# Attention scores at full height in two passes instead of half height in three, a rotated key copy and a joint last transpose

## The chip, the core and the metric

One core of a Trainium2 chip runs the whole program in one launch. The metric is the device time of one execution in microseconds (us). Engines: PE (TensorE, matmuls), DVE (VectorE), ACT (ScalarE), POOL (GpSimd), and SP (SyncE), which issues all DMAs here.

## The reference

Attention with a threshold, then two MLPs over the same 2304 tokens, all in fp32 (`q`, `k`, `v` are 4 x 8 x 576 x 64, the MLP weights 512 x 2048 and 2048 x 512):

```python
scores = scale * np.matmul(q, k.transpose(0, 1, 3, 2))
thresh = np.max(scores, axis=-1, keepdims=True) - tau
scores = np.where(scores >= thresh, scores, -1000000000.0)
...
attn = attn / (np.sum(attn, axis=-1, keepdims=True) + 1e-09)
return np.matmul(attn, v).astype(np.float32)
...
h = x @ w_in
g = np.maximum(h, 0.0) + alpha * np.minimum(h, 0.0)
...
h = x @ w_in
g = h - np.tanh(h)
```

The first MLP has the leaky step, the second `h - tanh(h)`; each ends with `g @ w_out`.

## The kernel before

**Precision.** Most matmuls take operands in a shorter format (`fp32r`). A value is written as a high part and a low part (the rest), and a product of two values is a sum of products of parts. The MLPs use three of the four products (L849 to L920).

**Visits.** Attention runs in 64 visits: for each of 4 batches, 256 queries of each of 8 heads (block 0), then the next 256 with the heads in reverse (block 1). The last 64 queries of two heads form one "left" tile, handled after every second visit of block 1 (`attend_left`, L723). `prep` (L407) loads and splits keys, values and queries of a visit; `attend` (L642) does the rest:

- *Scores* (`scores`, L649). The head dimension is 64, so a matmul contracts over 64 of 128 rows. The host lays keys and queries out twice, on rows 0 to 63 and 64 to 127; the upper half computes query tile 0 into the PSUM tile `sc0`, the lower half query tile 1 into `sc1`. A pass is 2 column chunks (320 and 256 keys) by 2 halves. Visits whose keys came with one of the first 22 visits (`raw`, `RAW` = 22) make a single pass in plain fp32; the other 42 make three passes (high x high, low x high, high x low), 12 matmuls.
- *Softmax* (`softmax`, L523): per tile row maximum (DVE), threshold, exponential (ACT), mask and sum (DVE), reciprocal, and a normalisation on ACT, DVE or POOL. The weights are in the tile `e`, 128 x 576, one per query tile.
- *Transposes* (`turned`, L581): four 128 x 128 transposes of a tile's first 512 keys into `pt` (`turn`, L587), copied out as high part (ACT) and low part (DVE); one transpose of the last 64 keys (`turn_last`, L591) into the first 128 columns of `sc0` or `sc1` (of `hp` in the first 8 visits).
- *Products* with the values (L668), then the sums that form the MLP's input.

The left tiles of raw heads use a two-head key tile and a zero-padded query tile `qz` (L736); the other left tiles use `qc` (L738), 8 matmuls on all 128 rows.

**MLPs.** Nine blocks of 256 tokens per layer, eight pairs of 128-wide hidden slices each: `h_pair` (L846) and `acc_pair` (L899). Layer 1 of a block begins when its eight visits are done and runs between later visits; layer 2 follows alone.

**Order.** All steps are recorded in a plan (`Plan`, L74) with engines, assumed costs, a rank, and what they read, write and take. `order` (L113) simulates the engines and issues, each time, the step that can start first; among steps ready at the same time the lower rank goes first. Where several engines are allowed, `ACT_PEN`, `DVE_PEN` and `POOL_PEN` are added to that engine's start. Each engine then runs its list in that order. 140 filler steps of two matmuls (`warm`, L974) have the last rank.

Ranks come from a visit's place times `TA` plus an offset by kind of step (`OFF`, L60):

```python
add({"PE": 1.27 if raw(k) else 1.09}, rank + OFF["S"], scores, ...
add({"PE": 0.434}, rank + OFF["T"], turn, [e0, ("const", 2), ROOM], [("pt", 0)], [("pt", 0)])
add({"PE": 0.07}, rank + OFF["T"], turn_last, [e0, ("const", 2), ROOM], [p5k], bank)
```

Of the kernel before, what the change touches and what calls it, by code (L numbers as in the profile page):

```python
# [22 lines left out]
P = 128  # L23
BLK = 256
# [5 lines left out]
KW, VW = S, 5 * D  # L30
QW = (BLK, BLK + D)
QH = P + D
# [5 lines left out]
TA = 13.2318  # L38
PA, PB = 19.265, 1.663
MLP_PE = 552.3152  # L40
MLP_G = -221.5201
PREP = 5.2216
# [4 lines left out]
POOL_PEN = 0.1711  # L47
ACT_PEN = 0.2206
# [6 lines left out]
XR = 58.2596  # L55
# [3 lines left out]
DVE_PEN = 0.7265  # L59
OFF = {"S": -61.66, "M": -127.29, "TH": -411.91, "E": -10.04, "X": -74.89, "R": -109.09, "N": 45.44, "T": 228.67, "H": -130.72, "L": -184.11, "AV": 77.62, "XC": -91.16, "XH": 81.73}  # L60
# [3 lines left out]
    "rkv": 1, "rq": 2, "ks": 3, "qs": 2, "vs": 3, "e": 3, "st": 2, "eT5": 1, "xt": 1, "rw": 4, "raw0": 2, "raw1": 4, "tw": 2,  # L64
# [165 lines left out]
def attention_mlp_mlp(ctx: ExitStack, tc: tile.TileContext, kv, q0, q1, tau, w1i, w1o, alpha, w2i, w2o, out):  # L230
# [30 lines left out]
    qc = tpool.tile([P, 2, P], F32R, name="qc")  # L261
    qz = tpool.tile([P, P], F32, name="qz")
# [115 lines left out]

# [28 lines left out]
    def prep(v, rank):  # L407
# [21 lines left out]

        def load_whole_k(e):  # L430
            T[ks] = take(tpool, ks, [P, 2, S], F32R, "ks", BUFS["ks"]).bitcast(F32)
            e.dma_start(out=T[ks][:, 0], in_=kv[b, h][:, :KW])

        def load_whole_v(e):
            x = take(tpool, vs, [P, 2, 5, D], F32, "vs", BUFS["vs"])
            e.dma_start(out=x[:, 0], in_=kv[b, h][:, KW:].rearrange("p (c d) -> p c d", c=5))
            T[vs] = x.rearrange("p a c d -> p c a d")
# [4 lines left out]

        def k_hi(e):
            copy(e, take(tpool, ks, [P, 2, S], F32R, "ks", BUFS["ks"])[:, 0], T[rkv][:, :KW])

        def k_lo(e):
            sub(e, T[ks][:, 1], T[rkv][:, :KW], T[ks][:, 0])
# [11 lines left out]
        def q_hi(e):  # L459
            x = take(tpool, qs, [P, 2, P], F32R, "qs", BUFS["qs"])  # L460
            copy(e, x.bitcast(F32)[:, 0] if raw(k) else x[:, 0], T[rq][:, :P], scale=qscale)

        def scaled_lo(e, lo, x, hi):
            e.scalar_tensor_tensor(
                out=lo, in0=x, scalar=qscale[P - lo.shape[0]:], in1=hi.bitcast(F32), op0=ALU.mult, op1=ALU.subtract
            )

        def q_lo(e):
            scaled_lo(e, T[qs][:, 1], T[rq][:, :P], T[qs][:, 0])
# [3 lines left out]

        half = HALVES[h % 2] if raw(k) else slice(0, P)

        def left_hi(e):
            copy(e, qz[half, col] if raw(k) else qc[:, h % 2, col], T[rq][half, P:], scale=qscale[half])

        def left_lo(e):
            x = qc[D:, h % 2, col]  # L480
            scaled_lo(e, x, T[rq][D:, P:], x)

        def load_two(e):
            x = take(tpool, kab, [P, KW + VW], F32, "rkv", BUFS["rkv"])
            for a in range(2):
                e.dma_start(out=x[HALVES[a], :KW], in_=kv[b, h + a][HALVES[a], :KW])

        add({"SYNC": rate * QH}, rank - 6, load_q, [ROOM], [rq], takes=[("rq", rq)], lag=DMA_LAG)
        k_raw, v_raw = (*rkv, 0), (*rkv, 1)
        if new:  # L490
# [10 lines left out]
            if not raw(k):  # L501
                add(any_of(0.58, 0.37, 0.64), rank, k_hi, [k_raw, ROOM], [(*ks, 0)], takes=[("ks", ks)])
                add(either(0.68, 1.42), rank, k_lo, [k_raw, (*ks, 0), ROOM], [(*ks, 1)])
        add({"ACT": 0.28}, rank, q_hi, [rq, ("const", 0), ROOM], [(*qs, 0)], takes=[("qs", qs)])
        if not raw(k):
            add({"DVE": 0.26}, rank, q_lo, [rq, (*qs, 0), ROOM], [(*qs, 1)])
        if qb:
            lc = ("qz" if raw(k) else "qc", 0, h % 2)
            if raw(k) and h % 2 == 0:
                add({"SYNC": rate * KW}, rank - 6, load_two, [ROOM], [(*kab, 0)], takes=[("rkv", kab)], lag=DMA_LAG)  # L510
            add({"ACT": 0.24}, rank, left_hi, [rq, ("const", 0), ROOM], [lc])
            if not raw(k):
                add({"DVE": 0.2}, rank, left_lo, [rq, ROOM], [lc])
# [9 lines left out]
    def softmax(tile, n, slots, rank):  # L523
# [4 lines left out]
        st = ("st", tile)  # L528
# [9 lines left out]
        def row_exp(e, j, s):  # L538
            e.activation(  # L539
                out=take(tpool, ("e", tile, j), [P, S], F32, "e", BUFS["e"]), in_=x(s), func=AF.Exp, bias=T[st][:, 0, j:j + 1], scale=1.0  # L540
            )

        def row_mask(e, j, s):
            w_ = T["e", tile, j]
# [10 lines left out]
        def normalise(e, j):  # L555
            w_, r = T["e", tile, j], T[st][:, 3, j:j + 1]
# [12 lines left out]
        add({"DVE": 0.13}, rank + OFF["TH"], threshold, [*[(*st, 0, j) for j in js], ("const", 0), ROOM], [(*st, 1)])  # L569
        for j, s in enumerate(slots):  # L570
            both = [("sc", s, 0), ("sc", s, 1)]
            ej = ("e", (tile, j))
            add({"ACT": 0.64}, rank + OFF["E"], lambda e, j=j, s=s: row_exp(e, j, s), [("sc", s, "s"), (*st, 0, j), ROOM], [ej], both, takes=[("e", ej)])
# [3 lines left out]
        for j in js:  # L577
            add({"ACT": 0.66, "DVE": 0.37, "POOL": 0.73}, rank + OFF["N"], lambda e, j=j: normalise(e, j), [(*st, 3), ROOM], [("e", (tile, j))])


    def turned(tile, j, s, rank, g, g5, w, left, half):  # L581

        cols = slice(0, P) if left else slice(j * P, (j + 1) * P)
        p5k, p5, bank = (("sc", s, "p5"), sc[s][:D, :P], [("sc", s, 0)]) if left or tile >= H else (("hp", s), hp[:D, s, :P], [("hp", 0)])
        e0 = ("e", (tile, j))

        def turn(e):  # L587
# [10 lines left out]
        def hi_last(e):  # L598
            if g5 not in T:
                take(tpool, g5, [P, BLK], F32R, "eT5", BUFS["eT5"])  # L600
            x = T[g5][half, cols].bitcast(F32) if w else T[g5][:D, cols]
            copy(e, x, p5)

        def lo_last(e):
            sub(e, T[g5][D:P, cols], p5, T[g5][:D, cols])

        def hi(e):
            if g not in T:
# [4 lines left out]
            if w:  # L613
                copy(e, x[:, :, cols].bitcast(F32), pt)
            elif left:
                copy(e, parts(x.rearrange("p c s -> p (c s)"), 0), pt.rearrange("p c (a s) -> p (c a) s", a=2))
            else:
                copy(e, x[:, :, cols], pt)

        def lo(e):  # L620
# [3 lines left out]
            else:  # L624
                sub(e, T[g][1][:, :, cols], pt, T[g][0][:, :, cols])

        first = j == 0
        add({"PE": 0.434}, rank + OFF["T"], turn, [e0, ("const", 2), ROOM], [("pt", 0)], [("pt", 0)])
        add({"PE": 0.07}, rank + OFF["T"], turn_last, [e0, ("const", 2), ROOM], [p5k], bank)
# [457 lines left out]
```

## Time and profile before

| | |
|---|---|
| median of 3 runs (lowest to highest) | 1180.67 us (1180.38 to 1181.76) |
| the profiled execution | 1180.95 us |
| its span (first to last instruction) | 1179.2 us |
| busy: PE, DVE, POOL, ACT | 1150.1, 678.1, 602.9, 575.0 us |
| chain that ended last, largest shares | PE 78%, DVE 11%, ACT 4% |
| DMA | 82.32 MB, mean 70 GB/s |

A busy time is the union of an engine's instructions, and idle time is put down to what ended it. Recorded durations of neighbouring matmuls overlap: the time that one takes of PE is the distance from its start to the next one's start, not its duration. Weight loads are a row of their own (PEld). Rows merge equal instructions that follow each other (x12) and name the first one's shape.

### The profile page before, as it was taken

What the parts mean: (1) busy time and instruction counts of PE and PEld (TensorE: products, weight loads), DVE (VectorE), ACT (ScalarE), POOL (GpSimd) and SP (SyncE); (2) the same over time, 40 slices, a digit from 0 to 9 for tenths busy, and PEclk for the clock granted to TensorE, in tenths of its full rate; (3) what the DMA queues carried; (4) which work ended last, traced back from release to release, by engine and by line L of the source; (5) the groups of instructions that cost most, each with busy time, mean ns of one, the idle gap of its engine ahead of it and who ended that gap; (6) DMA issues with size and microseconds to landing.
All of it is one profiled execution on the core that took longest, in us unless ns stands there. A gap on an engine that the chain in (4) does not pass through costs nothing.

```text
span 1179.2 us, 22125 instructions
## 1 busy us (share of the span) xinstructions
PE 1150.1 (98%) x8620; PEld 1049.2 (89%) x8620; DVE 678.1 (58%) x1388; ACT 575.0 (49%) x1132; POOL 602.9 (51%) x640
## 2 busy tenths in 40 slices
PE   9999999999999999999999999999999999999998
PEld 7777789899889898898998999998998999999997
DVE  5888887878877888878788685764111111111110
ACT  5877775666666656666665464564111111111111
POOL 3566655535556445555355377887344344344332
PEclk9999999999999999999999999999999999999999
DMA  6545432202122201121111153352011010010000
GB/s 192 181 151 165 150 103 73 58 24 60 39 59 90 58 25 55 43 91 55 42 41 55 41 186 134 127 162 90 1 36 37 1 37 27 11 36 7 13 19 18
DMA packets 51913, 82.32 MB, mean 70 GB/s; under 512 B 14688, under 2 KB 30048, under 8 KB 51808
## 3 DMA queue, kind: packets, MB, share of 16 engines
q1 hardware_dynamic: 51808, 80.91, 22.3%
q8 instruction: 68, 1.11, 0.4%
q14 instruction: 37, 0.30, 0.1%
HBM read 70.92 MB, written 9.96 MB: 69 GB/s over the span
## 4 chain that ended last, share of the span: by engine, by line
PE 78%; DVE 11%; ACT 4%; issue 3%; POOL 2%; DMA 1%; SPq 0%; ACTq 0%; DVEq 0%; POOLq 0%
PE hp L857 30%; PE acc L910 17%; PE acc L918 13%; PE sc L655 4%; PE pt L589 4%; PE sc L681 3%; DVE e L545 3%; DVE eT L285 2%; DVE st L533 1%; PE sc L592 1%; PE sc L771 1%; DVE st L550 1%; PE acc L673 1%; PE acc L976 1%; DMA rw<-in_w1i_dram 1%
## 5 line engine op out<-in xcount | busy, mean ns | idle before, releaser
L857 PE MATMUL hp<-x,ihi 128*128 128x256 f32 x2304 | 426.7, 285 | 1.0 <-POOL x L285 0.3
L857 PEld LDWEIGHTS hp<-x,ihi 128*128 128x128 f32 x2304 | 358.4, 189 | 9.3 <-issue 0.9
L857 PE MATMUL hp<-x,ilo 128*128 128x256 f32 x1152 | 324.0, 281 | 0.0
L876 DVE TENSOR_TENSOR mr<-hp,mr 128x512 f32<-128x512 f32 x72 | 49.8, 692 | 327.0 <-ACT mr L869 326.9
L857 PEld LDWEIGHTS hp<-x,ilo 128*128 128x128 f32 x1152 | 217.7, 189 | 0.0
L282 POOL TENSOR_SCALAR gh<-mr 128x512 fp32r<-128x512 f32 x100 | 63.3, 633 | 299.4 <-DVE mr L876 215.9
L285 POOL TENSOR_TENSOR gl<-mr,gh 128x512 fp32r<-128x512 f32 x144 | 192.5, 1337 | 21.2 <-ACT gh L280 13.6
L869 ACT ACTIVATE mr<-hp 128x512 f32<-128x512 f32 x72 | 43.1, 598 | 299.1 <-PE hp L857 295.5
L918 PE MATMUL acc<-gh,ohi 128*128 128x256 f32 x576 | 170.5, 296 | 0.0
L918 PE MATMUL acc<-gl,ohi 128*128 128x256 f32 x576 | 162.2, 282 | 0.0
L918 PE MATMUL acc<-gh,olo 128*128 128x256 f32 x576 | 161.9, 281 | 0.0
L533 DVE TENSOR_REDUCE st<-sc 128x1 f32<-128x576 f32 x144 | 106.3, 753 | 38.6 <-PE sc L655 23.1
L545 DVE SCALAR_TENSOR_TENSOR e<-sc,st,e 128x576 f32<-128x576 f32 x144 | 116.3, 814 | 12.3 <-ACT e L539 4.3
L539 ACT ACTIVATE e<-sc,st 128x576 f32<-128x576 f32 x144 | 105.2, 735 | 19.0 <-DVE st L533 16.9
L910 PE MATMUL acc<-ohi,gl 128*128 128x512 f32 x288 | 113.9, 395 | 0.0
L910 PE MATMUL acc<-olo,gh 128*128 128x512 f32 x288 | 113.8, 395 | 0.0
L910 PE MATMUL acc<-ohi,gh 128*128 128x512 f32 x288 | 113.5, 394 | 0.0
L918 PEld LDWEIGHTS acc<-gh,ohi 128*128 128x128 f32 x576 | 109.1, 189 | 1.8 <-issue 1.3
L918 PEld LDWEIGHTS acc<-gl,ohi 128*128 128x128 f32 x576 | 108.9, 189 | 0.1
L918 PEld LDWEIGHTS acc<-gh,olo 128*128 128x128 f32 x576 | 108.6, 189 | 0.0
L280 ACT ACTIVATE e<-e,st 128x576 f32<-128x576 f32 x97 | 72.9, 770 | 61.1 <-DVE st L553 60.1
L280 ACT ACTIVATE eT<-pt 128x512 fp32r<-128x512 f32 (+1 forms) x144 | 85.4, 593 | 30.6 <-PE pt L589 26.4
(89 smaller groups left out, 1953.0 us busy)
## 6 DMA issues: line engine op xcount, KB each, us to landing
rkv<-in_kv_dram SPq DMA_DIRECT2D x36, 288.0 KB, 2.8
rw<-in_w1i_dram SPq DMA_DIRECT2D x16, 512.0 KB, 4.5
rw<-in_w1o_dram SPq DMA_DIRECT2D x16, 512.0 KB, 4.2
rw<-in_w2i_dram SPq DMA_DIRECT2D x16, 512.0 KB, 4.6
rw<-in_w2o_dram SPq DMA_DIRECT2D x16, 512.0 KB, 3.4
rkv<-in_kv_dram SPq DMA_DIRECT2D x44, 160.0 KB, 2.8
ks<-in_kv_dram SPq DMA_DIRECT2D x20, 288.0 KB, 2.9
rq<-in_q_dram SPq DMA_DIRECT2D x160, 32.0 KB, 2.1
```

Of the source, the lines that this page charges most:

```text
L280: e.activation(out=out_, in_=in_, func=AF.Copy, **({} if scale is None else {"scale": scale}))
L282: e.tensor_scalar(out=out_, in0=in_, scalar1=1.0, scalar2=1.0, op0=ALU.mult, op1=ALU.mult)
L285: e.tensor_tensor(out=out_, in0=in_, in1=hi.bitcast(F32), op=ALU.subtract)
L533: e.tensor_reduce(out=T[st][:, 0, j:j + 1], in_=x(s), axis=AX.X, op=ALU.max, negate=True)
L539: e.activation(out=take(tpool, ("e", tile, j), [P, S], F32, "e", BUFS["e"]), in_=x(s), func=AF.Exp, bias=T[st][:, 0, j:j + 1], scale=1.0)
L545: e.scalar_tensor_tensor(out=w_, in0=x(s), scalar=T[st][:, 1, j:j + 1], in1=w_, op0=ALU.is_ge, op1=ALU.mult, accum_out=T[st][:, 2, j:j + 1])
L589: e.transpose(pt[:, c, :], T["e", tile, j][:, c * P:(c + 1) * P], ident)
L655: e.matmul(sc[j][:, 192:192 + S][:, c], lhsT=q_[p], rhs=k_[p, c], start=(n == 0), stop=(n == len(ops) - 1))
L857: e.matmul(hp[:, k, :], lhsT=weight(l, "i", part, f // 4)[:, c, (f % 4) * P:(f % 4 + 1) * P], rhs=T[f"x{x}", m][:, c, :], start=(n0 + n == ...
L876: e.tensor_tensor(out=T[r], in0=hp, in1=T[r], op=ALU.subtract)
L910: e.matmul(acc[t], lhsT=g[:, k, t * P:(t + 1) * P], rhs=w, start=(f == 0 and n == 0), stop=(f == NF - 1 and n == 2),)
L918: e.matmul(acc[t][:, (c % 2) * BLK:(c % 2 + 1) * BLK], lhsT=w[:, c * P:(c + 1) * P], rhs=g[:, k, :], start=(f == 0 and n == 0 and c % 2 == ...
```

## The change

**Scores of the 42 later visits.** The key tile no longer holds high and low parts side by side (`[P, 2, S]`) but stacked: high part on rows 0 to 63, low part on rows 64 to 127 (`k_lo` overwrites the lower half). A matmul on all 128 rows with the query's high part in both halves gives high x high plus high x low; a second pass with its low part gives the other two products. A query tile takes two passes of two chunks, 4 matmuls, and is a step of its own; a visit has 8 instead of 12. The query's high and low parts are formed for 256 columns instead of 128.

**Rotated keys.** The key tile has 640 columns: the last 64 keys, then all 576. Tile 1 of the queries reads columns 0 to 575, so its scores begin with the last 64 keys; tile 0 reads columns 64 to 639. The weights of both are neighbours in one tile `e` of 1152 columns, and the two pieces with the last 64 keys lie side by side: one 128-column transpose turns both. It needs both normalisations, and always goes to `sc0` (or `hp`). This holds for all 64 visits. The key load has a second DMA for the rotated 64 columns (for 56 loads), and the `e` buffers go from three of 576 columns to two of 1152.

**Left tiles.** Raw ones put their query tile behind the keys in the same buffer (four `memset`s on POOL, no `qz`); the others have stacked parts, still 8 matmuls.

**Ranks and assumed costs** are new, `ACT_PEN` becomes 0. By the two orders 89 of the copies of `gh` go from POOL to ACT (ACT 44 to 133, POOL 100 to 11), and some 50 other copies; DVE keeps 1246 instructions.

```diff
-TA = 13.2318
-PA, PB = 19.265, 1.663
...
-ACT_PEN = 0.2206
+TA = 16.6305
+PA, PB = 26.706, 2.665
...
+ACT_PEN = 0
...
+        def fill_k(e, x):
+            e.dma_start(out=x[:, D:KW], in_=kv[b, h][:, :S])
+            e.dma_start(out=x[:, :D], in_=kv[b, h][:, S - D:S])
...
         def k_lo(e):
-            sub(e, T[ks][:, 1], T[rkv][:, :KW], T[ks][:, 0])
+            sub(e, T[ks][D:], T[rkv][D:, :KW], T[ks][D:])
...
         def q_lo(e):
-            scaled_lo(e, T[qs][:, 1], T[rq][:, :P], T[qs][:, 0])
+            scaled_lo(e, T[qs][:, 1], T[rq][:, :BLK], T[qs][:, 0])
...
         def turn_last(e):
-            e.transpose(p5, T["e", tile, j][:, 4 * P:], ident)
+            e.transpose(p5, T[ek][:, 4 * P:4 * P + rows], ident)
...
-        add({"PE": 0.434}, rank + OFF["T"], turn, [e0, ("const", 2), ROOM], [("pt", 0)], [("pt", 0)])
-        add({"PE": 0.07}, rank + OFF["T"], turn_last, [e0, ("const", 2), ROOM], [p5k], bank)
...
+        for j in range(n):
+            add({"PE": 0.438}, rank + OFF["T"], lambda e, j=j: turn(e, j), [(*ek, j), ("const", 2), ROOM], [("pt", 0)], [("pt", 0)])
...
+        add({"PE": 0.111}, rank + OFF["T"], turn_last, [*[(*ek, j) for j in range(n)], ("const", 2), ROOM], [p5k], bank)
...
-                    for j, p in enumerate(HALVES):
-                        e.matmul(sc[j][:, 192:192 + S][:, c], lhsT=q_[p], rhs=k_[p, c], start=(n == 0), stop=(n == len(ops) - 1))
...
+        def scores(e, j):
+            for part in range(2):
                 for c in CHUNKS:
+                    e.matmul(
+                        sc[j][:, 192:192 + S][:, c], lhsT=T["qs", v][:, part, j * P:(j + 1) * P],
+                        rhs=T["ks", k][:, (1 - j) * D:][:, c], start=(part == 0), stop=(part == 1),
+                    )
```

PE, scores of a later visit. Before (L655; `sc_90` and `sc_91` are the PSUM tiles `sc0` and `sc1`, L918 is layer 1 of the MLP); the last four rows come three times in all:

```order
L918 MATMUL acc_92<-gh,olo_1849 128x256
L655 MATMUL sc_90<-ks,qs 128x320 [waits DVE_49]
L655 MATMUL sc_91<-ks,qs 128x320 [waits DVE_49,Activation_49]
L655 MATMUL sc_90<-ks,qs 128x256
L655 MATMUL sc_91<-ks,qs 128x256
```

Now, for another later visit (L689; `sc_89` and `sc_90` are `sc0` and `sc1`, L721 ends the products of an earlier visit, L896 is layer 1):

```order
L721 MATMUL sc_89<-eT_2958,vs 128x256
L689 MATMUL sc_89<-ks,qs 128x320
L689 MATMUL sc_89<-ks,qs 128x256
L689 MATMUL sc_89<-ks,qs 128x320
L689 MATMUL sc_89<-ks,qs 128x256
L689 MATMUL sc_90<-ks,qs 128x320 [waits DVE_49]
L689 MATMUL sc_90<-ks,qs 128x256
```

The two tiles' matmuls no longer alternate, and each tile waits for its own bank.

PE, transposes of the first visit. Before (L589 is `turn`, L592 `turn_last`, L976 the fillers):

```order
L589 MATMUL pt<-ident,e 128x128 [waits Activation_49]
L589 MATMUL pt<-ident,e 128x128 x3
L592 MATMUL hp<-ident,e 64x128
L976 MATMUL acc_93<-qc 128x256 x2
L592 MATMUL hp<-ident,e 64x128 [waits Activation_49]
L976 MATMUL acc_93<-qc 128x256 x6
L589 MATMUL pt<-ident,e 128x128 [waits Activation_49]
L589 MATMUL pt<-ident,e 128x128 x3
```

Now (L615 is `turn`, L618 `turn_last`, L1014 the fillers):

```order
L615 MATMUL pt<-ident,e 128x128 [waits Activation_49]
L615 MATMUL pt<-ident,e 128x128 x3
L618 MATMUL hp<-ident,e 128x128 [waits Pool_49]
L1014 MATMUL acc_92<-qc 128x256 x8
L615 MATMUL pt<-ident,e 128x128 [waits Activation_49]
L615 MATMUL pt<-ident,e 128x128 x3
```

One last-key transpose is left, with the second tile's normalisation (here on POOL) as its wait. In the new order it stands between the two tiles' transposes in 52 of 64 visits, in 24 of them directly behind the first tile's.

SP, the first loads. Before (L420 queries, L432 keys, L436 values, L322 weights of layer 1):

```order
L949 DMA tau_sb<-in_tau_dram 128x1
L973 DMA alpha_sb<-in_alpha_dram 128x16x1
L420 DMA rq<-in_q_dram 64x128 x2
L432 DMA ks<-in_kv_dram 128x576
L436 DMA vs<-in_kv_dram 128x320
L322 DMA rw<-in_w1i_dram 128x1024 x2
```

Now (L421 queries, L427 and L428 keys, L442 values, L320 weights):

```order
L988 DMA tau_sb<-in_tau_dram 128x1
L421 DMA rq<-in_q_dram 64x128 x2
L427 DMA ks<-in_kv_dram 128x576
L428 DMA ks<-in_kv_dram 128x64
L442 DMA vs<-in_kv_dram 128x320
L1011 DMA alpha_sb<-in_alpha_dram 128x16x1
L421 DMA rq<-in_q_dram 64x128 x2
L427 DMA ks<-in_kv_dram 128x576
L428 DMA ks<-in_kv_dram 128x64
L442 DMA vs<-in_kv_dram 128x320
L320 DMA rw<-in_w1i_dram 128x1024 x2
```

The first weights now stand behind the loads of two visits.

## Rows read from the trace of the kernel before

**Rows 1.** The page, busy time of PE and the granted clock in 40 slices.

```profile
PE 1150.1 (98%) x8620; PEld 1049.2 (89%) x8620; DVE 678.1 (58%) x1388; ACT 575.0 (49%) x1132; POOL 602.9 (51%) x640
...
PEclk9999999999999999999999999999999999999999
```

**Rows 2.** Busy time in four stretches: us, then each engine (instructions), clock, DMA.

```profile
0.00:140.00 140.00, 135.25 (x918) 106.09 (x918) 108.97 (x205) 101.28 (x208) 80.02 (x91) 1.00 0.55 167
140.00:224.00 84.00, 81.75 (x653) 73.98 (x653) 67.73 (x148) 57.59 (x120) 47.49 (x53) 1.00 0.30 90
224.00:674.00 450.00, 433.79 (x3684) 409.97 (x3684) 364.90 (x868) 282.37 (x585) 230.88 (x279) 1.00 0.18 52
674.00:1179.00 505.00, 499.29 (x3371) 459.19 (x3369) 136.56 (x169) 133.77 (x221) 244.51 (x218) 1.00 0.17 55
```

**Rows 3.** Groups by form: count, busy us, mean ns; idle us before them, and releasers.

```profile
L589 PE MATMUL pt<-ident,e 128*128 128x128 f32 x576 | 88.9, 277 | 7.3 <-ACT e L280 4.7 <-POOL e L560 1.2 <-ACT eT L280 0.5
...
L589 PEld LDWEIGHTS pt<-ident,e 128*128 128x128 f32 x576 | 64.4, 140 | 17.5 <-ACT e L280 8.8 <-issue 2.4 <-POOL e L560 2.4
...
L592 PE MATMUL sc<-ident,e 128*64 128x128 f32 x128 | 31.5, 280 | 8.5 <-ACT xt L280 5.9 <-DVE pair L801 0.9 <-DVE xt L695 0.3
...
L592 PEld LDWEIGHTS sc<-ident,e 128*64 128x64 f32 x128 | 12.9, 110 | 16.9 <-ACT xt L280 12.0 <-DVE pair L801 1.5 <-ACT e L280 1.2
```

**Rows 4.** Stretches again, first L976 alone, then L655 alone.

```profile
0.00:140.00 140.00, 43.19 (x280) 37.77 (x280) 1.00 0.55 167
...
0.00:140.00 140.00, 17.39 (x112) 9.78 (x112) 1.00 0.55 167
```

**Rows 5.** Chain that ended last: start us, length us, what; one row of layer 1.

```profile
677.31 2.84 PE hp L857 x24
```

**Rows 6.** PE in order of time around one score block: start us, length us.

```profile
266.38 0.28 PE L918 MATMUL acc<-gh,olo 128*128 128x256 f32 x1
266.58 1.07 PE L655 MATMUL sc<-ks,qs 64*128 64x320 f32 x12
267.58 0.38 PE L918 MATMUL acc<-gh,ohi 128*128 128x256 f32 x1
267.80 0.28 PE L918 MATMUL acc<-gl,ohi 128*128 128x256 f32 x1
```

**Rows 7.** PE in order of time around one block of L741.

```profile
258.57 0.28 PE L918 MATMUL acc<-gh,olo 128*128 128x256 f32 x1
258.69 1.23 PE L741 MATMUL sc<-ks,qc 128*128 128x320 f32 x8
259.76 0.40 PE L857 MATMUL hp<-x,ihi 128*128 128x256 f32 x2
```

**Rows 8.** PE in order of time around two last-key transposes in a row.

```profile
421.58 0.28 PE L857 MATMUL hp<-x,ilo 128*128 128x256 f32 x1
421.70 0.38 PE L592 MATMUL sc<-ident,e 128*64 128x128 f32 x2
421.84 0.48 PE L857 MATMUL hp<-x,ihi 128*128 128x256 f32 x2
422.16 0.28 PE L857 MATMUL hp<-x,ilo 128*128 128x256 f32 x1
```

**Rows 9.** SP's issues and PE at the start, in order of time.

```profile
4.12 0.59 SPq L432 DMA_DIRECT2D ks<-in_kv_dram  x1
...
7.48 1.24 PE L655 MATMUL sc<-ks,qs 64*128 64x320 f32 x8 [0.50 <-DMA ks<-in_kv_dram]
```

**Rows 10.** Groups by form, the low part of q on DVE, two shapes.

```profile
L464 DVE SCALAR_TENSOR_TENSOR qs<-rq,qscale,qs 128x128 fp32r<-128x128 f32 x42 | 18.9, 450 | 2.8 <-ACT qs L280 2.8
...
L464 DVE SCALAR_TENSOR_TENSOR qc<-rq,qscale,qc 64x64 fp32r<-64x64 f32 x24 | 8.7, 364 | 0.8
```

**Rows 11.** Groups by form, the normalisation on ACT and on POOL.

```profile
L280 ACT ACTIVATE e<-e,st 128x576 f32<-128x576 f32 x97 | 72.9, 770 | 61.1 <-DVE st L553 60.1
...
L560 POOL TENSOR_SCALAR e<-e,st 128x576 f32<-128x576 f32 x47 | 36.4, 774 | 46.9 <-DVE st L553 44.6 <-PE acc L673 1.9 <-DMA rkv<-in_kv_dram 0.4
```

More of the change, by code (lines that the diff above doesn't have):

```diff
@@ L54 @@
 GRP = 2
-XR = 58.2596
+XR = 138.8108
 FLEX = 1
@@ L526, in x, with weights @@
             return sc[s][:, 192:192 + S]
-        st = ("st", tile)
+        st, ek = ("st", tile), ("e", tile)
+        def weights(j):
+            return T[ek][:, j * S:(j + 1) * S]
         def row_max(e, j, s):
@@ L538, in row_exp @@
         def row_exp(e, j, s):
-            e.activation(
-                out=take(tpool, ("e", tile, j), [P, S], F32, "e", BUFS["e"]), in_=x(s), func=AF.Exp, bias=T[st][:, 0, j:j + 1], scale=1.0
-            )
+            if not j:
+                take(tpool, ek, [P, 2 * S], F32, "e", BUFS["e"])
+            e.activation(out=weights(j), in_=x(s), func=AF.Exp, bias=T[st][:, 0, j:j + 1], scale=1.0)
         def row_mask(e, j, s):
-            w_ = T["e", tile, j]
+            w_ = weights(j)
             e.scalar_tensor_tensor(
@@ L577, in softmax, with turned, cols, turn @@
         for j in js:
[L578 to L587, printed above, removed]
+            add({"ACT": 0.66, "DVE": 0.37, "POOL": 0.73}, rank + OFF["N"], lambda e, j=j: normalise(e, j), [(*st, 3), ROOM], [(*ek, j)])
+    def turned(tile, slots, rank, g, g5, w, left, half):
+        n, s, ek = len(slots), slots[0], ("e", tile)
+        rows = n * D
+        p5k, p5, bank = (("sc", s, "p5"), sc[s][:rows, :P], [("sc", s, 0)]) if left or tile >= H else (("hp", tile % 2), hp[:rows, tile % 2, :P], [("hp", 0)])
+        def cols(j):
+            return slice(j * P, (j + 1) * P)
+        def turn(e, j):
+            x = T[ek][:, j * (S + D):][:, :4 * P]
             for c in range(4):
-                e.transpose(pt[:, c, :], T["e", tile, j][:, c * P:(c + 1) * P], ident)
+                e.transpose(pt[:, c, :], x[:, c * P:(c + 1) * P], ident)
         def turn_last(e):
-            e.transpose(p5, T["e", tile, j][:, 4 * P:], ident)
+            e.transpose(p5, T[ek][:, 4 * P:4 * P + rows], ident)
         def parts(x, n):
@@ L971, in attention_mlp_mlp @@
     add({"DVE": 0.3}, -100, scales, [], [("const", 0)])
-    add({"POOL": 0.46}, 0, clear, [], [("const", 1)] + [(x, 0, a) for x in ("qc", "qz") for a in range(2)])
+    add({"POOL": 0.46}, 0, clear, [], [("const", 1)] + [("qc", 0, a, part) for a in range(2) for part in range(2)])
     add({"SYNC": 0.3}, -1, lambda e: e.dma_start(out=alpha_sb, in_=alpha.rearrange("(f p) -> p f", p=P)), [], [("alpha", 0)], lag=2.5)
```

186 lines of the change are left out of this document (101 added, 85 removed).

## The prediction

> **What bounds the kernel now.** First the page's busy shares and slices: TensorE (PE) is busy 1150.1 of 1179.2 us, 98%, at a granted clock of nine tenths or more in every slice, so at its upper level of 2.4 GHz throughout [rows 1]. Then the stretches: PE is full in all four, and the nearest other engine is VectorE (DVE), 364.9 of 450 us (81%) between 224 and 674 us, where the attention visits run between the matmuls of layer 1 [rows 2]. So time is gained by fewer PE microseconds or fewer PE waits. PE idles 29.1 us in all; the transposes account for over half of it: 8.5 us ahead of the 64-column ones (L592) and 7.3 us ahead of the 128-column ones (L589) [rows 3].
>
> One exception: 280 filler matmuls (L976), all before 140 us, keep PE busy while the visits wait for other engines [rows 4]. Their number is fixed, so PE work saved among them need not shorten anything. 112 recorded score matmuls lie there, at 8 a visit 14 of the 22 early visits.
>
> PE's durations of one instruction overlap, so I price PE work by distances between starts. The step of an ordinary 256-column matmul is 2.84/24 = 0.118 us [rows 5].
>
> **Score blocks, 42 of 64 visits.** (The 22 early visits keep their single pass; their blocks are the same size.) Now a block is 12 matmuls on half the rows. From the last matmul ahead of one (266.38) to the second behind it (267.80) are 1.42 us; two ordinary steps are 0.236, so the block costs 1.184 us [rows 6]. The twelve run as six pairs, but the block shows a penalty at both edges: its first matmul starts 0.20 us after the one ahead, and the second behind it 0.22 us after the first, where a step is 0.118. The new block is 8 matmuls on all rows, four of 320 and four of 256 columns. The leftover rows' scores (L741) have exactly that form today: 258.57 to 259.76 is 1.19 us, less one step 1.07 us [rows 7]. Gain 0.114 us, times 42: **4.8 us**. Bounds: the block may lose its good fit when split into two halves of four (nothing gained, 0), or save what the rows say; nothing in them gives more.
>
> The Trainium skill has a rule against this. "TensorEngine Tiling (Array Packing)", section "Theoretical Speedup", promises up to twice the speed for a contraction of 64 rows or fewer, so by it giving up the half-height form is a loss (rival 4 has the time). The same page's "Key Properties" says that a switch of mode drains the engine; the two edges agree with that, and the block measured in place, 1.184 us against 1.07, decides.
>
> **Last-key transposes, 64 visits.** A full visit has two 64-column transposes (L592), in future one of 128 columns; the order has 144 such instructions before and 80 after. Two in a row: from 421.58 to 422.16 are 0.58 us, less three steps of 0.118 leaves 0.226, or 0.113 us each [rows 8]. The new one loads 128 columns of weights, 0.140 against 0.110 us [rows 3]; that load lies beside the matmul ahead, so I add nothing, with 0.03 x 64 = 1.9 us as the bound. All 64 would give 7.2 us; the 14 visits among the fillers I leave out, so 50 x 0.113 = **5.6 us**.
>
> **Waits at that transpose.** PE idles 8.5 us ahead of the 128 L592 that write the score banks, mostly released by ScalarE (ACT) [rows 3]: 0.066 us each. Of these 56 go (the other 16 become 8), which would save 3.7. But each remaining one needs both halves of the weights normalised, and behind it on PE's queue stand fillers or MLP matmuls and the other half's transposes. I take half, **1.9 us**; the ends are a gain of 8.5 and the loss in the first rival.
>
> **Queues at the start.** Each key load gains a second, 64-column DMA on SyncE (SP). The alpha load moves behind the first visit, and the first w1i load behind the second visit's four. A key load holds SP 0.59 us, and the first scores waited for exactly this DMA [rows 9]. The later alpha load gives some of that back. I add **0.5 us**. If the later weights reach the end the price is the second visit's five issues, at 0.59 each some 3 us; but the first MLP matmul still stands behind nine visits in both orders, and from the eighth weight piece on the loads stand behind about the same visits. Lower end 0.
>
> **Moved or lengthened elsewhere, taken as nothing.** On DVE the low part of q is 256 columns instead of 128 (42 times). From 64 rows by 64 columns to 128 by 128 the same operation goes from 364 to 450 ns [rows 10], so 64 more columns are 86 ns and 128 more some 0.17 us: 7.2 us on DVE in a stretch with 85 us free. GpSimd (POOL) subtracts half as many key rows but 11% more columns; it has over 200 us free in that stretch. The shift from POOL to ACT (89 copies of gh among others) fills an engine with 168 us free from 224 to 674 and 371 afterwards [rows 2]. The cover in each case is PE's backlog of MLP matmuls: 786 layer-1 matmuls before and 810 now, at 0.118 us some 93 and 96 us, stand behind the last attention work in the order. Without it, these would surface as PE waits (second rival). Splitting the scores per tile lets slot 0's maximum start half a block sooner; that shortens a chain that PE mostly does not wait for, so nothing.
>
> **Sum.** The profiled execution took 1180.95 us (span 1179.2 and 1.75 around it), 0.28 above the median of 1180.67. 1180.95 - 4.8 - 5.6 - 1.9 + 0.5 = 1169.15; against the median **1168.9 us**. This case by itself: 1160 (all transposes count, every L592 wait goes) to 1175 (no gain in waits, 3 us lost at the start, longer weight loads).
>
> **Rivals.**
> 1. *Slower: the single transpose waits for the second half.* In 52 of 64 visits the new order puts it between the two halves' transposes. A normalisation lasts 0.770 us on ACT or 0.774 on POOL [rows 11]; when one engine does both, the second half is ready 0.77 us after the first, while the first half's four transposes take 0.44 (four at 0.11). That is a wait of 0.33 us, times 52 = 17 us: 1180.7 - 4.8 - 5.6 + 0.5 + 17.2 = 1188. It decides from a mean of 0.19 us per visit. For: 24 of them stand directly behind the first half's transposes. Against: in the others matmuls stand between, and normalisations run on two engines at once. 0.08.
> 2. *The gain turns into idle time.* If the visits are paced by the softmax chain on DVE, the stretch stays 450 us and PE waits instead. Only the eight visits between fillers and 224 us gain 0.113 each, 0.9: 1180.7 + 0.5 - 0.9 = 1180.3. For: 81% DVE, and 7 us more. Against: PE itself waits for it rarely [rows 3]. 0.06.
> 3. *The new order also removes waits.* If the 15.8 us ahead of both kinds of transposes vanish instead of 1.9, 1180.7 - 4.8 - 5.6 - 15.8 + 0.5 = 1155. For: slots are free separately, and the weights' buffers hold two whole visits instead of one and a half. Against: the producers are as busy as before. 0.14.
> 4. *Slower: half-height pairs are cheaper than full height.* If each of the six pairs cost one full-height step of 1.07/8 = 0.134 us [rows 7], the block would cost 0.80 us and the change would add 0.27, times 42 = 11.3 us: 1180.7 - 5.6 - 1.9 + 0.5 + 11.3 = 1185. The block measured in place, edges and all, speaks against it [rows 6]. 0.02. This is what the Trainium skill's rule above would do here.
>
> **How the numbers follow.** A measurement of this kernel tells about 0.2%, 2.4 us, from no change. My forecast has 0.70. Faster: forecast and rival 3, 0.84. Same: rival 2, 0.06. Slower: rivals 1 and 4, 0.10. The range 1157 to 1178 takes in the forecast's own bounds and most of rival 3, and leaves out rivals 1, 2 and 4 and the end of 3, about 0.19.
>
> **What would show it.** Right: a non-early score block of 1.07 us without longer steps at its edges, 80 last-key transposes at 0.11 us, PE idle time at or below 29 us, attention ending some 10 us earlier and everything after 674 us merely shifted. Wrong: idle time ahead of the new transpose released by a normalisation (rival 1), idle time spread over the score blocks' successors with DVE near 90% (rival 2), or blocks above 1.15 us (rival 4).

## The result, and the profile after the change

| | before | after |
|---|---|---|
| median of the comparison (lowest to highest) | 1181.17 us (1180.38 to 1181.76) | 1169.38 us (1168.69 to 1170.11) |
| ratio, 95% interval | | 0.9901 [0.9884, 0.9918] |
| profiled execution, span | 1180.95, 1179.2 us | 1169.88, 1168.1 us |
| PE busy, and idle (span less busy) | 1150.1, 29.1 us | 1141.2, 26.9 us |

The time is 11.8 us shorter; 1168.9 was forecast. First the page of the changed kernel, busy time (share of the span, instructions) and granted clock; it answers to [rows 1].

```profile
PE 1141.2 (98%) x8388; PEld 1051.9 (90%) x8388; DVE 662.9 (57%) x1388; ACT 663.6 (57%) x1277; POOL 525.5 (45%) x498
...
PEclk9999999999999999999999999999999999999999
```

PE has 8.9 us less work and 2.2 us less idle time. DVE has 15 us less, with the same 1388 instructions. The stretches, as in [rows 2] (us, then PE, PEld, DVE, ACT, POOL, clock, DMA):

```profile
0.00:140.00 140.00, 131.51 (x887) 102.27 (x887) 106.52 (x202) 105.48 (x213) 69.67 (x80) 1.00 0.58 171
...
224.00:674.00 450.00, 437.74 (x3567) 425.93 (x3568) 362.50 (x877) 318.62 (x647) 222.54 (x240) 1.00 0.23 65
```

Groups by form on PE, as in [rows 3] (count, busy us, mean ns, idle us ahead of them and releasers). L615 answers to L589, L618 to L592, L689 to the later visits' part of L655.

```profile
L615 PE MATMUL pt<-ident,e 128*128 128x128 f32 x576 | 88.6, 276 | 6.4 <-ACT e L278 2.2 <-ACT eT L278 2.1 <-DVE eT L283 1.4
L689 PE MATMUL sc<-ks,qs 128*128 128x320 f32 x168 | 49.8, 322 | 3.4 <-DVE xt L734 2.3 <-DVE e L565 0.9 <-ACT eT L278 0.2
...
L618 PE MATMUL sc<-ident,e 128*128 128x128 f32 x56 | 16.4, 293 | 5.6 <-ACT xt L278 3.4 <-DVE xt L734 1.4 <-ACT pair L278 0.3
...
L618 PE MATMUL sc<-ident,e 128*64 128x128 f32 x16 | 4.4, 274 | 0.0
```

The last-key transposes in the score banks wait 5.6 us in all, for 56 + 16 of them, where 128 waited 8.5 us. Their releasers are the steps that take an earlier visit's products out of the bank (`xt`, `pair`); the normalisation of the weights is not among those shown. The score blocks, which before waited 0.5 us in all, now wait 3.4, mostly until DVE has added up the products that lie in the same bank. Together that is 9.0 us, and 8.5 + 0.5 = 9.0 before. One score block, as in [rows 6] and [rows 7]:

```profile
357.99 0.28 PE L896 MATMUL hp<-x,ilo 128*128 128x256 f32 x1
358.11 1.23 PE L689 MATMUL sc<-ks,qs 128*128 128x320 f32 x8
359.18 0.40 PE L896 MATMUL hp<-x,ihi 128*128 128x256 f32 x2
```

1.19 us less one step is 1.07: the block costs what was forecast, and the long steps at its edges are gone. One joint transpose among matmuls of layer 1, as in [rows 8]:

```profile
239.93 0.28 PE L957 MATMUL acc<-gh,olo 128*128 128x256 f32 x1
240.05 0.27 PE L618 MATMUL sc<-ident,e 128*128 128x128 f32 x1
240.08 0.37 PE L957 MATMUL acc<-gh,ohi 128*128 128x256 f32 x1
240.28 0.28 PE L957 MATMUL acc<-gl,ohi 128*128 128x256 f32 x1
```

From 239.93 to 240.28 are 0.35 us; less two steps of 0.118 this leaves 0.114 us, and 0.113 was forecast. The attention ends earlier too; these are the last products of the left tiles, before and after (last number of the two: start of the last one):

```profile
L771 PE MATMUL sc<-eT,vs x190: 218/272/328, 98.6 to 672.7; 128*128 128x128 f32 x104, 128*64 128x64 f32 x48, 128*128 128x64 f32 x26, 64*64 64x64 f32 x12
```

```profile
L810 PE MATMUL sc<-eT,vs x190: 218/270/327, 99.0 to 660.4; 128*128 128x128 f32 x104, 128*64 128x64 f32 x48, 128*128 128x64 f32 x26, 64*64 64x64 f32 x12
```

So far every sign that the prediction named is there: 1.07 us blocks, 80 transposes, less idle time, an end of attention 12.3 us earlier. From these two traces alone the forecast looks right in its steps too. The experiments say otherwise.

### The profile page after: what moved, and what is told of

Read it like the earlier page. It is cut to its first block, busy times and chain, and to the rows that moved or that the text cites. A ratio compares the mean times of both kernels' runs of the same rounds, so it can differ in the third digit from the quotient of the medians.

```text
span 1168.1 us, 21647 instructions
## 1 busy us (share of the span) xinstructions
PE 1141.2 (98%) x8388; PEld 1051.9 (90%) x8388; DVE 662.9 (57%) x1388; ACT 663.6 (57%) x1277; POOL 525.5 (45%) x498
## 4 chain that ended last, share of the span: by engine, by line
PE 72%; DVE 15%; ACT 8%; issue 3%; DMA 2%; SPq 1%; POOL 0%; DVEq 0%; ACTq 0%; POOLq 0%
PE hp L896 29%; PE acc L949 17%; PE acc L957 11%; PE sc L720 3%; DVE e L565 3%; PE pt L615 3%; DVE eT L283 3%; PE sc L689 2%; DVE st L553 2%; DMA rw<-in_w1i_dram 2%; ACT eT L278 1%; ACT e L561 1%; DVE st L570 1%; PE sc L681 1%; DVE mr L917 1%
## 5 line engine op out<-in xcount | busy, mean ns | idle before, releaser
L896 PE MATMUL hp<-x,ihi 128*128 128x256 f32 x2304 | 426.4, 284 | 1.7 <-DVE mr L917 1.6
L896 PEld LDWEIGHTS hp<-x,ihi 128*128 128x128 f32 x2304 | 358.9, 189 | 9.3 <-issue 1.4
L896 PE MATMUL hp<-x,ilo 128*128 128x256 f32 x1152 | 323.9, 281 | 0.0
L896 PEld LDWEIGHTS hp<-x,ilo 128*128 128x128 f32 x1152 | 217.5, 189 | 0.0
L278 ACT ACTIVATE gh<-mr 128x512 fp32r<-128x512 f32 x133 | 83.8, 630 | 73.9 <-DVE mr L915 48.8
L615 PE MATMUL pt<-ident,e 128*128 128x128 f32 x576 | 88.6, 276 | 6.4 <-ACT e L278 2.2
```

Of the source, the lines that this page charges most:

```text
L278: e.activation(out=out_, in_=in_, func=AF.Copy, **({} if scale is None else {"scale": scale}))
L615: e.transpose(pt[:, c, :], x[:, c * P:(c + 1) * P], ident)
L896: e.matmul(hp[:, k, :], lhsT=weight(l, "i", part, f // 4)[:, c, (f % 4) * P:(f % 4 + 1) * P], rhs=T[f"x{x}", m][:, c, :], start=(n0 + n == ...
```

## The experiments

All ratios are against the kernel before, timed on the same chip. The idle time of PE is the span less PE's busy time.

### One part of the change alone, nothing else moved

Three kernels take PE work out of the kernel before and leave every other instruction where it is. The first has full-height scores (8 matmuls instead of 12 in the 42 blocks; the operands stay the half-height ones, so the scores aren't the reference's):

```diff
+            if not raw(k):
+                for j in range(2):
+                    for part in range(2):
+                        for c in CHUNKS:
+                            e.matmul(sc[j][:, 192:192 + S][:, c], lhsT=qs[:, part], rhs=ks[:, part, c], start=(part == 0), stop=(part == 1))
+                return
```

> The kernel before, its plan and order on every engine untouched; only the 42 later score blocks are issued as 8 full-height matmuls instead of 12 half-height ones, on the old operand layout (so those scores are not the reference's). Theory (PE work saved in a stretch that PE bounds passes to the end one for one): 42 x 0.114 = 4.8 us less than before, block 1.07 us by the starts around it. Rival (the gain of the change came from the new order and its ranks, PE work is covered): no change, within 1 us of before.

Measured: 1180.17 us, ratio 0.999 [0.9981, 0.9999], that is 1.2 us of the 4.8 (the interval allows 0.1 to 2.2).

```profile
L589 PE MATMUL pt<-ident,e 128*128 128x128 f32 x576 | 88.9, 277 | 8.3 <-ACT e L280 5.4 <-POOL e L560 1.5 <-DVE eT L285 0.5
...
L592 PE MATMUL sc<-ident,e 128*64 128x128 f32 x128 | 31.5, 279 | 8.8 <-ACT xt L280 5.9 <-DVE pair L807 0.9 <-DVE st L533 0.5
```

The waits at the transposes grew by 1.0 and 0.3 us against [rows 3]. Set against the trace of before, instruction by instruction in the same order, PE gains about 0.1 us at a block, is up to 0.85 us ahead, and gives most of it back at transposes that wait for normalised weights. The next kernel makes one 128-column last-key transpose per visit (taken from the first tile alone, so the second tile's last keys are not turned; the copies read the two halves of its output):

```diff
...
-            e.transpose(p5, T["e", tile, j][:, 4 * P:], ident)
+            if left:
+                e.transpose(p5, T["e", tile, j][:, 4 * P:], ident)
+            elif j == 0:
+                e.transpose(both5, T["e", tile, j][:, S - P:], ident)
```

> The kernel before, plan and order untouched; in a full visit the first last-key transpose is 128 columns wide and the second is not issued, the copies read the two halves of its output (the second half's last keys are not the reference's, and nothing waits for both normalisations). Theory: 50 x 0.113 = 5.6 us less than before, because the 14 visits among the fillers give nothing; 7.2 us if they count too. Rival (gain from the order): no change. If the waits ahead of this transpose halve as well, up to 4 us more.

Measured: 1186.05 us, ratio 1.0043 [1.0029, 1.0056]: 4.7 us slower.

```profile
L661 PE MATMUL sc<-ks,qs 64*128 64x320 f32 x340 | 59.6, 377 | 4.0 <-DVE e L545 2.8 <-DMA ks<-in_kv_dram 1.0
...
L598 PE MATMUL sc<-ident,e 128*128 128x128 f32 x56 | 16.8, 299 | 6.8 <-ACT xt L280 3.6 <-DVE pair L807 2.0 <-DVE xt L701 0.4
L596 PE MATMUL sc<-ident,e 128*64 128x128 f32 x16 | 4.6, 286 | 2.3 <-ACT xt L280 2.3
```

The 56 + 16 transposes that are left wait 9.1 us, more than the 128 did, and the scores 4.0 instead of 0.5; PE's idle time is 35.4 us (span 1183.7) instead of 29.1. Both halves now lie in one bank. The releasers are steps that read that bank in the old order: the copies and sums of products (`xt`, `pair`) and the mask of the softmax (L545). The third kernel has both edits:

> Both edits of the two runs before it on the kernel before, order untouched (same parts of the output change). Theory: the two gains add, 10.4 us less than before, 12.0 if the early visits count. Rival (order): no change. If one gain hides behind the other: clearly less than the sum of the two runs.

Measured: 1186.1 us, ratio 1.0038 [1.0026, 1.0051]. On top of the joint transpose the cheaper scores gave nothing.

### The new numbers alone

The kernel before with the block of constants of the change (ranks, fits, penalties), its code untouched:

```diff
...
-MLP_PE = 552.3152
+MLP_PE = 1031.4114
...
-POOL_PEN = 0.1711
-ACT_PEN = 0.2206
+POOL_PEN = 0.1305
+ACT_PEN = 0
...
-DVE_PEN = 0.7265
+DVE_PEN = 0.9665
...
```

> The kernel before, planned with the new ranks and engine penalties (the constants alone; assumed costs, tiles and instructions as before). Theory: the order is worth at most the waits, so between 3 us less and 3 us more than before. Rival (the gain came from the order): some 11 us less.

Measured: 1171.09 us, ratio 0.9905 [0.989, 0.992]. This kernel still has twelve half-height matmuls a block and two last-key transposes a visit, and it is 10.3 us faster. The page and the groups on PE:

```profile
PE 1147.7 (98%) x8620; PEld 1047.9 (90%) x8620; DVE 652.6 (56%) x1388; ACT 645.5 (55%) x1264; POOL 525.9 (45%) x508
```

```profile
L589 PE MATMUL pt<-ident,e 128*128 128x128 f32 x576 | 88.8, 277 | 4.7 <-ACT e L280 2.1 <-ACT eT L280 0.9 <-DVE eT L285 0.7
L655 PE MATMUL sc<-ks,qs 64*128 64x320 f32 x340 | 58.3, 378 | 0.1
...
L592 PE MATMUL sc<-ident,e 128*64 128x128 f32 x128 | 32.0, 279 | 5.9 <-ACT xt L280 3.8 <-ACT e L539 0.9 <-POOL vs L285 0.4
```

PE idles 22.9 us instead of 29.1, and of these 6.2 us 2.6 each are at L589 and L592. From here on three theories stand against each other. **Theory A**: the gain is POOL's shorter list (POOL 603 to 526 us busy, small DVE operations shorter), so that the softmax chain is quicker. **Theory C**: it is the order. **Theory B**, the prediction's, was left to show that the new structure gives something by itself.

### The parts of the numbers, and the structure without them

The changed kernel with the old constants:

```diff
...
-MLP_PE = 1031.4114
+MLP_PE = 552.3152
...
-ACT_PEN = 0
+ACT_PEN = 0.2206
...
```

> The changed kernel with the constants of the kernel before (ranks, fits and penalties): the new structure alone, both parts of it, in an order planned from the old numbers; the result is the reference's. Theory A (the 10 us that the new numbers alone gave came from moving work off POOL, and PE work that is taken away turns into waits as it did in the full-height scores with the order untouched): 1178 to 1182 us, within 0.3% of before, with PE busy some 9 us below before and PE idle 6 to 9 us above it. Theory B (the prediction's: PE work saved passes to the end): 1169 to 1171 us, PE idle near 29 us as before.

Measured: 1180.19 us, ratio 0.9995 [0.9986, 1.0004], as theory A has it and not B. Its page, groups by form on PE, stretches (us, PE busy, granted clock, DMA), and the wait in them (L896 answers to L857 of the kernel before, L810 to L771):

```profile
PE 1142.2 (97%) x8388; PEld 1053.1 (89%) x8388; DVE 665.0 (57%) x1388; ACT 576.1 (49%) x1120; POOL 619.9 (53%) x655
```

```profile
L896 PE MATMUL hp<-x,ihi 128*128 128x256 f32 x2304 | 428.0, 285 | 7.5 <-DVE mr L917 4.5 <-ACT eT L278 2.1 <-POOL x L283 0.4
...
L689 PE MATMUL sc<-ks,qs 128*128 128x320 f32 x168 | 50.6, 327 | 2.2 <-DVE e L565 0.9 <-POOL ks L283 0.6 <-DVE xt L734 0.5
...
L810 PE MATMUL sc<-eT,vs 128*128 128x128 f32 x104 | 16.8, 282 | 4.0 <-DVE eT L283 3.2 <-DVE e L565 0.7
L618 PE MATMUL sc<-ident,e 128*128 128x128 f32 x56 | 16.1, 287 | 3.1 <-DVE xt L734 1.7 <-ACT xt L278 1.1 <-DVE pair L840 0.2
...
L618 PE MATMUL sc<-ident,e 128*64 128x128 f32 x16 | 4.5, 280 | 2.5 <-DVE xt L734 1.7 <-ACT xt L278 0.4
```

```profile
500.00:504.00 4.00, 3.47 (x25) 1.00 0.50 151
504.00:508.00 4.00, 2.19 (x12) 0.89 0.24 75
508.00:512.00 4.00, 4.00 (x26) 0.69 0.27 71
```

```profile
505.79 1.62 PE L810 MATMUL sc<-eT,vs 128*128 128x128 f32 x10 [2.21 <-DVE eT L283]
```

PE's work is down 7.9 us, and its idle time up 5.6 to 34.7. The last-key transposes wait less, 3.1 + 2.5 = 5.6 us against 8.5. What grew are the waits ahead of matmuls that the change doesn't touch: the MLP's (L896) 7.5 us against 1.0 before, the products of the left tiles (L810) 4.0 against 0.0. One wait of 2.21 us for DVE does double damage: behind it the granted clock is at its lower level (1.2 GHz) for part of the next 8 us, which by the shares of the clock costs another 0.11 x 4 + 0.31 x 4 = 1.7 us, an estimate.

Next the two halves of the numbers. Penalties alone:

```diff
-POOL_PEN = 0.1711
-ACT_PEN = 0.2206
+POOL_PEN = 0.1305
+ACT_PEN = 0
...
-DVE_PEN = 0.7265
+DVE_PEN = 0.9665
```

> The kernel before with only the three penalties of the change (POOL_PEN 0.1305, ACT_PEN 0, DVE_PEN 0.9665): all ranks and all fits stay, but 94 of the 100 gh copies and some 50 other operations go from POOL to ACT (POOL 645 to 497 instructions, ACT 1134 to 1282). The result is the reference's. Theory A (the gain of the new numbers comes from POOL's shorter list: small DVE operations get shorter where POOL is still, so the softmax chain that paces the visits gets shorter): most of the 10.3 us, 1171 to 1174 us, with the 128x2 threshold on DVE near 380 ns instead of 480 and PE idle near 23 us. Theory C (the gain comes from the order that the new ranks give): 1179 to 1182 us, even if DVE's operations are shorter.

Ranks and fits alone are the rest of that block, with the three lines left as they were:

> The kernel before with all the new numbers except the three penalties, which stay as they were: the new order, with POOL's list as long as before (639 instructions, 99 gh copies on it). The result is the reference's. Theory A (POOL's list is what counts): 1179 to 1182 us, the threshold on DVE near 480 ns as before. Theory C (the order is what counts): 1170 to 1174 us with the threshold still near 480 ns.

Measured: penalties alone 1176.68 us, ratio 0.9963 [0.9951, 0.9976]; ranks alone 1182.5 us, ratio 1.001 [1.0001, 1.002]. Neither theory had this: 4.4 faster and 1.5 slower make 10.3 faster together. The page with the penalties alone:

```profile
PE 1148.4 (98%) x8620; PEld 1049.7 (89%) x8620; DVE 660.7 (56%) x1388; ACT 661.9 (56%) x1280; POOL 512.3 (44%) x492
```

Theory A falls on DVE's rows, of before, of ranks alone and of all the new numbers in the old kernel (count, busy us, mean ns):

```profile
L536 DVE TENSOR_SCALAR st<-st,atau 128x2 f32<-128x2 f32 x64 | 30.7, 480 | 1.0
L550 DVE TENSOR_SCALAR st<-st 128x2 f32<-128x2 f32 x64 | 29.9, 467 | 1.5
```

```profile
L536 DVE TENSOR_SCALAR st<-st,atau 128x2 f32<-128x2 f32 x64 | 25.1, 392 | 1.0
L550 DVE TENSOR_SCALAR st<-st 128x2 f32<-128x2 f32 x64 | 17.6, 275 | 0.9
```

```profile
L536 DVE TENSOR_SCALAR st<-st,atau 128x2 f32<-128x2 f32 x64 | 23.8, 371 | 1.1
L550 DVE TENSOR_SCALAR st<-st 128x2 f32<-128x2 f32 x64 | 20.5, 320 | 0.9
```

With ranks alone POOL is as busy as before (600.5 us) and these operations are nearly as short as with all the new numbers, in the slowest of the three. With penalties alone POOL is busy 512.3 us, and they last 338 and 406 ns. So POOL's load as a whole does not set their length, and their length does not set the time. Part of what does, with ranks alone, are single stalls again:

```profile
504.01 2.29 PE L771 MATMUL sc<-eT,vs 128*128 128x128 f32 x9 [1.82 <-DVE eT L285]
```

```profile
500.00:504.00 4.00, 2.19 (x19) 1.00 0.43 141
504.00:508.00 4.00, 3.99 (x18) 0.52 0.03 2
508.00:512.00 4.00, 4.00 (x27) 0.62 0.36 114
```

After a wait of 1.82 us come 8 us at a mean clock of 0.52 and 0.62, which by the same estimate is 3.4 us more. Between 660 and 680 us the clock falls once more (0.91 over these 20 us, another 1.8). Together that is about the 5.2 us by which PE is busier than with all the new numbers (1152.9 us against 1147.7); its idle time is 4.6 us longer (27.5 against 22.9). The timed runs agree: nine of eleven had a mean clock of 0.994 or 0.995 and took 1181.8 us or more; the two at 0.998 and 1.0 took 1179.80 and 1178.79. Even those two are some 8 us slower than the kernel with all the new numbers (1171.09), so the lower clock is less than half of the difference. The Trainium skill, "TensorE: Matmul & The Clock Gate", section "What's actually happening", says that the throttle is the default and activity releases it. The trace agrees: the clock fell behind the wait of 1.82 us and rose again while PE was busy (3.99 and 4.00 of 4.00 us at 0.52 and 0.62).

The next kernel puts the full-height scores of the first experiment into the kernel with the new numbers:

> The kernel before with all the new numbers (it took 1171.1 us), its order untouched, and in it the 42 non-raw score blocks issued as 8 full-height matmuls instead of the twelve; the operands are the half-height ones, so the scores are not the reference's. Each block costs 0.114 us less on PE. If PE is the bound once the softmax chain is quicker: 1166 to 1168 us. If the visits still wait for the chain, as in the same edit under the old numbers (-1.2 us): 1169.5 to 1171 us, with PE idle up by about 4 us.

Measured: 1169.44 us, ratio 0.9903 [0.9889, 0.9916]. The median is 1.7 us below the kernel with the new numbers alone, the ratio only 0.0002 (0.2 us), and the intervals overlap: between nothing and some 3 us, less than the 4.8 of the block's price. The wait that was to swallow the rest does not show, though:

```profile
PE 1143.4 (98%) x8452; PEld 1055.9 (91%) x8452; DVE 651.4 (56%) x1388; ACT 645.1 (55%) x1264; POOL 526.0 (45%) x508
```

PE idles 23.0 us (span 1166.4) against 22.9, and is busy 4.3 us less. These two profiles are the fastest execution of this kernel and the slowest of the other, so how much of the block's price reaches the end here stays open.

### Does PE work count in the changed kernel?

> The changed kernel once more, on the chip and beside the runs of before that the next three are compared with: 1168 to 1171 us, ratio near 0.990 as in the first comparison, granted clock 0.999 or above.

Measured: 1169.39 us, ratio 0.9903 [0.9889, 0.9916]. Two kernels were timed beside it. The first leaves out the joint transpose of the later visits, the second issues it three times:

```diff
+            if left or tile < 18:
                 e.transpose(p5, T[ek][:, 4 * P:4 * P + rows], ident)
```

> The changed kernel, its order untouched, without the joint last-key transpose of the 46 visits from the 19th on (the copies read what the tile last held, so the weights of the last 64 keys are not the reference's). That takes 46 x 0.113 = 5.2 us of work off PE and one link out of the chain from the normalised weights to the products. Theory 'PE is the bound' (as predicted): 5 us less than the changed kernel, 1164.5 us. Theory 'what PE saves turns into waits when nothing else moves' (full-height scores with the order untouched gave 1.2 of 4.8 us under the old numbers and 1.7 under the new): 1 to 2 us less, 1167.5 to 1168.5 us, with PE idle up by 3 to 4 us.

```diff
+            for _ in range(3 if not left and tile >= 14 else 1):
                 e.transpose(p5, T[ek][:, 4 * P:4 * P + rows], ident)
```

> The changed kernel, its order untouched, with the joint last-key transpose of the 50 visits from the 15th on issued three times: 100 x 0.113 = 11.3 us more work on PE at the very place of the edit, and 0.2 us more on the chain of each visit; the result is the reference's. If PE is the bound: 1180 to 1182 us. If PE has slack there that the added work can fill: 1172 to 1176 us. Together with the run that takes these transposes away it shows whether PE work counts the same in both directions.

Measured: 1164.96 us, ratio 0.987 [0.9857, 0.9884], for 46 transposes fewer, and 1178.42 us, ratio 0.9979 [0.997, 0.9988], for 100 more. That is 4.4 us less (0.096 each) and 9.0 more (0.090 each), about the same both ways, four fifths of the 0.113 that was taken from the rows. The first agrees with "PE is the bound"; the second lies 1.6 us below that theory's range and 2.4 above its rival's. The pages of the two, and of the changed kernel beside them:

```profile
PE 1136.7 (98%) x8342; PEld 1047.4 (90%) x8342; DVE 662.7 (57%) x1388; ACT 664.0 (57%) x1277; POOL 524.8 (45%) x498
```

```profile
PE 1151.1 (98%) x8488; PEld 1063.2 (90%) x8488; DVE 662.0 (56%) x1388; ACT 663.8 (56%) x1277; POOL 524.8 (45%) x498
```

```profile
PE 1140.8 (98%) x8388; PEld 1052.5 (90%) x8388; DVE 662.6 (57%) x1388; ACT 664.1 (57%) x1277; POOL 525.2 (45%) x498
```

PE's idle time stays within 24.8 to 26.1 us (spans 1162.8, 1176.3 and 1165.6): here most of the saved work passes, and the idle time as a whole doesn't grow.

The last corner, structure and penalties with the old ranks (the three lines of the penalties, put into the changed kernel with old constants):

> The changed kernel with the old ranks and fits but the new penalties: the corner that is missing of structure, ranks and penalties. So far, against before: structure alone -0.9 us, penalties alone -4.4, ranks alone +1.5, ranks and penalties -10.3, all three -11.8. If the parts add up: 1175.5 to 1176.5 us. If the structure's saved PE work passes once the plan leaves no long stall (structure alone lost 5.9 us at one wait near 505 us, with PE's clock at half for some us behind it, after leading by 5.2 us): about 1171 us, with no stretch of PE below a granted clock of 1.0 in its profile. If a new stall of that kind stands in it: 1176 us or above.

Measured: 1173.18 us, ratio 0.9934 [0.9921, 0.9948], between the first two values, and the stall is there, at another place. Its page, the wait, and the stretches around it:

```profile
PE 1143.9 (98%) x8388; PEld 1054.4 (90%) x8388; DVE 665.1 (57%) x1388; ACT 661.4 (56%) x1273; POOL 526.7 (45%) x502
```


```profile
182.18 0.96 PE L615 MATMUL pt<-ident,e 128*128 128x128 f32 x4 [2.25 <-DVE eT L283]
```

```profile
180.00:184.00 4.00, 1.82 (x10) 0.80 0.24 75
184.00:188.00 4.00, 4.00 (x17) 0.50 0.00 0
188.00:192.00 4.00, 3.77 (x26) 0.85 0.54 156
```

The lower clock costs 0.20 x 4 + 0.50 x 4 + 0.15 x 4 = 3.4 us here, by the same estimate. Against penalties alone (1176.68 us, ratio 0.9963) the structure is worth 3.5 us, and PE's idle time is the same: 27.5 us (span 1171.4) and 27.7 (span 1176.1).

## Why the number was right and two of its steps were not

Six profiles make a ledger, in us: PE's busy and idle time, and the median with its ratio.

| | PE busy | PE idle | median | ratio |
|---|---|---|---|---|
| before | 1150.1 | 29.1 | 1181 | |
| new structure, old numbers | 1142.2 | 34.7 | 1180.19 | 0.9995 |
| old structure, new numbers | 1147.7 | 22.9 | 1171.09 | 0.9905 |
| old structure, penalties alone | 1148.4 | 27.7 | 1176.68 | 0.9963 |
| new structure, penalties alone | 1143.9 | 27.5 | 1173.18 | 0.9934 |
| both (the change) | 1141.2 | 26.9 | 1169.38 | 0.9901 |

By its columns the structure takes 7.9 us of work off PE and adds 5.6 of idle time under the old numbers, 6.5 and 4.0 under the new ones, and takes 4.5 and 0.2 under the penalties alone. The numbers take 2.4 or 1.0 of work and 6.2 or 7.8 of idle time. (The forecast had 10.4 us of work and 1.9 of waits for the structure.) These are single executions: a second profile of the changed kernel has 24.8 us of idle time instead of 26.9, and work at the lower clock counts as busy. On the medians the structure is worth 0.9, 1.7 and 3.5 us instead of the forecast's 11.8; under the new numbers the two ratios, 0.9905 and 0.9901, can't be told apart.

- **Score blocks, -4.8.** The price of the block is right (1.07 us). That all of it reaches the end is not shown: 1.2 us alone under the old numbers, 0 to 3 by the times under the new.
- **Last-key transposes, -5.6.** The price holds (0.114 us in place). What reaches the end of the changed kernel is 0.090 to 0.096 us each, so 50 are 4.5 to 4.8. With the old order untouched the joint transpose cost 4.7 us instead of gaining.
- **Waits at that transpose, -1.9; beside this term lies the first step that failed.** The term itself holds, with 8.5 us before and 5.6 both in the changed kernel and with the structure alone. What failed is that no other wait was to grow, so that the saved work would reach the end. In the changed kernel the score blocks take back what the transposes lost (9.0 us for both, before and after). With the structure alone PE idles 5.6 us more, above all ahead of the MLP's matmuls (7.5 us instead of 1.0) and the left tiles' products (4.0 instead of 0.0).
- **Start, +0.5.** No run isolates it. The first scores start earlier (5.89 us; 7.48 in [rows 9]), but PE is busy 131.5 of the first 140 us instead of 135.3, part of which is work that went.
- **"Moved or lengthened elsewhere, taken as nothing": the second step that failed, and the larger.** The engine shift and the new order were costed as instructions that find cover. They were looked at as a plan that has fewer waits only in the third rival, and alone they give 10.3 of the 11.8 us. The two errors are of about one size and opposite signs. That the sum came out is luck.

Of the **rivals**, the first (single transpose waits for the second half) does not show in the changed kernel: the waits there are 5.6 us and not 17, and nearly all of them end with a step that empties the bank, none of those shown with a normalisation. The second, gain turned into idle time, is near what the structure does under the old numbers (-0.9 us on the median, 5.6 us more idle), though DVE is no busier than before: it is late at single places, not full. The third, that the new order removes waits, was right as a mechanism and too hopeful in size: the numbers alone take 5.2 of the 15.8 us at both kinds of transposes, and the structure gives part of that back. The fourth is excluded by the block.

What stays open: which of the ranks matters, and why the old plan stalls at just those places. The structure with the new ranks and the old penalties wasn't tried. That the stalls and the lower clock explain part of the sum of penalties and ranks is argued from the profiles, not shown by a run that removes only the stalls. None of the kernels beats the changed one with all of the work done.

## What to carry to other kernels

When a change comes with new numbers for a planner, time the old code with the new numbers and the new code with the old ones before believing any step: here a sum that agreed within 0.5 us hid two errors of some 8 to 11 us. A price from distances between starts holds for the instruction; whether it reaches the end depends on what the next instruction in that order waits for, and taking away a transpose with its place in the plan kept (four fifths arrived) is another thing than merging two that write different banks (slower until the order was redone). And look at the granted clock in stretches of a few us where a kernel that should be faster is not: in the structure with old numbers the 40 slices show only nines.

## What the runs showed of the hardware that was not expected

Single PE waits of 1.82, 2.21 and 2.25 us in the middle of dense work were followed by the lower clock level and 1.7 to 3.4 us more, 0.8 to 1.9 times the wait. Not every such wait does it: the structure with the old numbers also waits 1.85 us at 187.5 us, the changed kernel 1.88 us at 16.5 us, and the clock stays at 1.00. With ranks alone it fell to 0.64 (672 to 676 us) behind a wait of only 1.30 us. So the length of the one wait doesn't decide.

Two-column operations on DVE (L536, L550) lasted 275 to 480 ns on average, with 148 to 214 ns for one column. The spread is in single instances, of the kernel before (min/median/max ns over both widths):

```profile
L550 DVE TENSOR_SCALAR st<-st x80: 143/170/1359, 15.1 to 666.1; 128x2 f32<-128x2 f32 x64, 128x1 f32<-128x1 f32 x16
```

The Trainium skill, "SBUF — State Buffer", section "SBUF: two separate sides", says that DVE and GpSimd lock a shared port pair for a whole instruction and the other side blocks. It says this of DVE operations in a two-port mode, or with two SBUF inputs while GpSimd reads SBUF; no row tells whether L550 is one of them. Instances of up to 1.36 us would fit such a lock. But the mean was 406 ns with POOL busy 512.3 us and 275 ns with 600.5, no run here isolates it, and it did not decide the time.
